# Narrow blocks of the first expert folded in three separate steps, and another order for the second expert's splits and the last index product

## The chip, the core and the metric

The kernel runs on one core of one Trainium2 chip. The metric is the device time of one execution in microseconds (us). The core's engines are TensorE (PE; its weight loads are listed as PEld), VectorE (DVE), ScalarE (ACT), GpSimd (POOL) and SyncE (SP). Each engine works through its own queue in the order in which the program gave the instructions out; engines wait for each other by semaphores.

## What is computed

Two stages: an attention with decay over 4 batches and 8 heads of 576 positions by 64, and on its 2304 rows of 512 a mixture of 8 experts in which each row goes to one expert.

```python
ret = scale * (q @ k.T) * Dmat            # Dmat: gamma_h ** (i - j), lower triangle
x = (ret @ v) as rows of 8 * 64
logits = x @ w_gate
e = argmax(logits); gate_w = softmax(logits)[e]
slot = position among the rows of expert e   # at most 2 * 2304 / 8 = 576
h = relu(rows_of_e @ w1[e])               # 512 -> 1024
y = h @ w2[e]                             # 1024 -> 512
out[row] = gate_w * y[its slot]
```

## The kernel before

**Two stages on one queue of work.** The attention runs over 18 tiles of 128 rows. Routing is computed in four groups of tiles (4, 4, 5 and 5): logits, the best expert (DVE: `lg`, `mx`, `cand`, `first`, `ohs`), ranks within experts (PE), then an index product (PE, L538, from `hot` and `vals` into the bank `psl`) that makes the list of rows of each expert, and a weight product (PE, L596, from `hot` and `wals`) that makes the list of gate weights. The last group's routing is interleaved with the first expert. The order of all instructions is written out by hand: a manual schedule keeps the order in which the code gives them out, and each engine keeps that order in its own queue.

**Precision.** A weight or activation is held as two f16 numbers, a high and a low part (`wh` and `wl`, `hh` and `hl`), and each product is made of three matmuls: high by high, high by low, low by high.

**Weights.** An expert has four quarters of 1 MB, loaded by SP (L238, `fetch`) into four buffers `raw`. Each quarter is split in two halves: `high` is an activation on ACT (L262, writes `wh`), `low` an operation on DVE (L270, writes `wl`, 128x1024). When `low` of a quarter's second half has been given out, the buffer's next load is given out behind it. An expert thus has eight parts 0 to 7; the text calls a `high` and a `low` of one part a split.

**One expert** (`run`). Eight blocks f of 12 matmuls (L901 to L903) each fill one of three rotating PSUM banks `ph`; ACT writes `hh` from it (L906), DVE `hl` (L907). Then `full(r)` multiplies 128 rows at a time (24 matmuls, L927 to L929, one of four rotating banks `py`; ACT scales to `ot`, L914, and POOL scatters the rows to the output, L918). The rest of less than 128 rows goes to `narrow(r, n)`: matmuls with 64 or 32 columns (L947) write partial sums into different partitions of two banks x and y. Its result must be folded: ACT copies from y to `both` and `more` (L996 to L1002), DVE adds x and `both` (L1003) and `more` (L1004), then ACT scales to `ot` (L1007, L1009) and POOL scatters. How many rows an expert has is known at run time only; `sized` chooses among widths by branches (L700).

**The order of experts.** Expert 0 comes in two parts: its first 256 slots (one `full` and one `narrow` of 128) while the last routing is under way, and its second part (112 slots, one `narrow`). Experts 1 to 7 follow. What else is to be given out during `run` stands in a table `pieces`: the key (f,) means behind block f (from 0), the key (r, f) behind step f of the product of row block r. The table of the first part gives out, among others, the routing steps `go` (routing of the last group; the last one of them is the last index product), `rows_late` (gathers of expert 0's second part and of expert 1, ranks), `w1st` and `w2nd` (gate weights of the last two groups), and the `hi` and `lo` of expert 1. `turn_late` transposes the second part's rows: ACT copies one half to `exT`, DVE the other (L1071). Expert 2's splits during expert 1, and later ones, follow `SPLITS_AT`.

**Held output.** For expert 0's first part `run` gets a list `held`: the scaling and scattering of its rows need the gate weights, which come late. `held` collects these steps (one for `full`, one for `narrow`), and `let_go`, given out behind block 4 of the second part, runs them all. The copies and additions of the fold itself are given out at once behind the narrow block.

Of the kernel before, what the change touches and what calls it, by code (L numbers as in the profile page):

```python
# [10 lines left out]
F32 = mybir.dt.float32  # L11
# [7 lines left out]
P = 128  # L19
# [20 lines left out]
    ((2,), (3,), (4,), (5,), (6,), (7,), (0, 3), (1, 3)),  # L40
# [3 lines left out]
HALF = 64  # L44
# [42 lines left out]
def retention_moe(ctx, tc, q, k, v, w_gate, w1, w2, capacity, consts, where, out):  # L87
# [796 lines left out]
    def run(w, xT, c0, T, pieces, idc, wtc, held=None, used=None, widths=(), at=1):  # L884
# [53 lines left out]
        def narrow(r, n):  # L938
# [52 lines left out]
            both = ob_p.tile([P, DM], F32, tag="both", name="both", bufs=1)  # L991
            more = ob_p.tile([P, DM], F32, tag="more", name="more", bufs=1)
            ot = ob_p.tile([P, DM], F32, tag="ot", name="ot")
            few = min(n, HALF)
            part = min(n, HALF + QUARTER)
            nc.scalar.copy(both[:few], y[HALF:HALF + few])  # L996
            if n > HALF:
                a, z = HALF, part
                nc.scalar.copy(both[a:z], y[0:z - a])  # L999
            else:  # L1000
                a, z = 0, min(n, QUARTER)
            nc.scalar.copy(more[a:z], y[QUARTER:QUARTER + z - a])  # L1002
            nc.vector.tensor_tensor(out=both[:part], in0=x[:part], in1=both[:part], op=ALU.add)  # L1003
            nc.vector.tensor_tensor(out=both[a:z], in0=both[a:z], in1=more[a:z], op=ALU.add)  # L1004

            def leave():
                nc.scalar.activation(ot[:part], both[:part], AF.Copy, scale=wtc(r)[:part])  # L1007
                if n > part:
                    nc.scalar.activation(ot[part:n], x[part:n], AF.Copy, scale=wtc(r)[part:n])  # L1009
                send(r, n, ot)  # L1010

            if held is None:
                leave()
            else:
                held.append(leave)
# [29 lines left out]
    def hi(*parts):  # L1045
        return sp(1, *parts, do=high)
# [30 lines left out]
    def let_go():  # L1077
        while held:
            held.pop(0)()
# [6 lines left out]
    for bank in phs.banks[:2]:  # L1086
# [3 lines left out]
               lambda: low(0, 2, 1), fetch, fetch],  # L1090
        (1,): [lambda: cross(NTI - 1, pys.banks[-1]), lambda: logits(NTI - 2)],
# [4 lines left out]
        (7,): [go, rows_late, w1st, w1st],  # L1096
        (0, 0): hi(0),
        (0, 1): hi(1, 2),
        (0, 2): hi(3),
        (0, 3): hi(4) + [w2nd],  # L1100
# [3 lines left out]
        (0, 7): [turn_late, w1st, w2nd] + hi(5) + lo(1),  # L1104
# [3 lines left out]
        (1,): lo(2),  # L1108
# [3 lines left out]
        (5,): lo(3),  # L1112
        (6,): [w2nd],
        (7,): hi(6),
        (0, 3): lo(4) + hi(7),
        (0, 7): lo(5),
    })
    rest = {(0,): lo(6), (1,): lo(7)}
    for e in range(1, E):
        pieces = {(p,): [] for p in range(KF)}  # L1120
        if e == 1:
            pieces.update(rest)
# [107 lines left out]
```

## Time and profile before

| | |
|---|---|
| median of 3 runs | 330.56 us (330.53 to 330.68) |
| the profiled execution | 332.88 us |
| its span, first to last instruction | 331.0 us |
| mean granted TensorE clock | 0.988 |
| PE / PEld busy | 308.3 / 216.6 us |
| DVE / ACT / POOL busy | 195.8 / 188.6 / 108.3 us |
| moved by DMA | 69.03 MB |

Busy time is the union of an engine's instructions; that of PE is modelled from pipelined matmuls. PE is busy for 93% of the span, so the question of each stretch is what ends its few idle times. The attention fills the time up to about 109 us, expert 0's first part with the last routing 109 to 130.5, its second part 130.5 to 142.8, expert 1 to 173.5, and the other six experts follow.

### The profile page before, as it was taken

What the parts mean: (1) busy time and instruction counts of PE and PEld (TensorE: products, weight loads), DVE (VectorE), ACT (ScalarE), POOL (GpSimd) and SP (SyncE); (2) the same over time, 40 slices, a digit from 0 to 9 for tenths busy, and PEclk for the clock granted to TensorE, in tenths of its full rate; (3) what the DMA queues carried; (4) which work ended last, traced back from release to release, by engine and by line L of the source; (5) the groups of instructions that cost most, each with busy time, mean ns of one, the idle gap of its engine ahead of it and who ended that gap; (6) DMA issues with size and microseconds to landing.
All of it is one profiled execution on the core that took longest, in us unless ns stands there. A gap on an engine that the chain in (4) does not pass through costs nothing. (4 is left out here: it accounts for less than half of the span.)

```text
span 331.0 us, 8265 instructions
## 1 busy us (share of the span) xinstructions
PE 308.3 (93%) x3227; PEld 216.6 (65%) x3228; DVE 195.8 (59%) x416; ACT 188.6 (57%) x333; POOL 108.3 (33%) x116
## 2 busy tenths in 40 slices
PE   8889999999998899779999999999999999999960
PEld 4678999899978775546447547647646647648620
DVE  4435587988579789759818815915914934912300
ACT  2567776876668466647557637736735736733310
POOL 1375353565409513116015012512414212421120
PEclk9999999999999999999999999999999999999995
DMA  8999999999967887986997993966995995721010
GB/s 176 197 200 218 273 247 267 233 231 244 239 222 159 286 321 156 221 268 201 217 327 228 305 260 120 357 151 227 363 208 201 293 191 209 154 58 38 3 36 33
DMA packets 97514, 69.03 MB, mean 209 GB/s; under 512 B 79975, under 2 KB 80359, under 8 KB 97456
## 3 DMA queue, kind: packets, MB, share of 16 engines
q1 hardware_dynamic: 93728, 58.08, 68.1%
q0 software_dynamic: 3728, 10.13, 8.9%
q8 instruction: 42, 0.69, 0.9%
q14 instruction: 16, 0.13, 0.1%
HBM read 53.58 MB, written 10.05 MB: 192 GB/s over the span
## 5 line engine op out<-in xcount | busy, mean ns | idle before, releaser
L270 DVE SCALAR_TENSOR_TENSOR wl<-raw,wh 128x1024 f16<-128x1024 f32 x62 | 76.9, 1241 | 8.6 <-ACT wh L262 8.1
L903 PE MATMUL ph<-exT,wl 128*128 128x296 f16 (+6 forms) x288 | 78.2, 278 | 1.7 <-issue 1.7
L901 PE MATMUL ph<-exT,wh 128*128 128x296 f16 (+6 forms) x288 | 78.2, 278 | 1.4 <-DVE hl L907 1.3
L902 PE MATMUL ph<-exT,wh 128*128 128x296 f16 (+6 forms) x288 | 78.2, 278 | 0.0
L918 POOL DMA_INDIRECT out<-ot,idx x24 | 26.0, 1084 | 140.9 <-ACT ot L914 75.3
L262 ACT ACTIVATE wh<-raw 128x1024 f16<-128x1024 f32 x64 | 66.6, 1052 | 1.6 <-DMA raw<-in_w 1.5
L907 DVE SCALAR_TENSOR_TENSOR hl<-ph,hh 128x256 f16<-128x256 f32 (+8 forms) x72 | 32.3, 453 | 36.2 <-ACT hh L906 36.1
L906 ACT ACTIVATE hh<-ph 128x256 f16<-128x256 f32 (+8 forms) x72 | 29.0, 411 | 29.9 <-PE ph L903 25.2
L927 PE MATMUL py<-wh,hh 128*128 128x512 f16 x120 | 45.5, 380 | 0.2 <-PEq L700 0.2
L929 PE MATMUL py<-wh,hl 128*128 128x512 f16 x120 | 45.5, 379 | 0.0
L928 PE MATMUL py<-wl,hh 128*128 128x512 f16 x120 | 45.5, 379 | 0.0
L901 PEld LDWEIGHTS <-wh 128*128 128x128 f16 x288 | 28.2, 98 | 10.4 <-issue 3.3
L902 PEld LDWEIGHTS <-wh 128*128 128x128 f16 x288 | 28.2, 98 | 8.7 <-issue 1.7
L903 PEld LDWEIGHTS <-wl 128*128 128x128 f16 x288 | 28.2, 98 | 6.5
L734 POOL DMA_INDIRECT xg<-xr,idx x24 | 28.0, 1167 | 12.4 <-issue 5.8
L914 ACT ACTIVATE ot<-py,sws 128x512 f32<-128x512 f32 x14 | 9.6, 687 | 39.3 <-PE py L929 31.6
L282 POOL TENSOR_TENSOR ks<-kn,cst 128x512 f32<-128x512 f32 x17 | 17.9, 1051 | 40.1 <-DMA kn<-in_k 31.8
L1003 DVE TENSOR_TENSOR both<-py,both 96x512 f32<-96x512 f32 (+6 forms) x9 | 6.2, 684 | 33.9 <-ACT both L999 19.0
L333 DVE TENSOR_TENSOR pm<-pp,cst 128x512 f32<-128x512 f32 x36 | 23.2, 684 | 2.5 <-PE pp L328 1.1
L947 PE MATMUL py<-wl,hh 128*64 128x512 f16 (+2 forms) x80 | 23.0, 381 | 0.0
L947 PE MATMUL py<-wh,hl 128*64 128x512 f16 (+2 forms) x80 | 22.0, 380 | 0.3 <-DVE hl L907 0.2
L947 PE MATMUL py<-wh,hh 128*64 128x512 f16 (+2 forms) x80 | 22.3, 382 | 0.0
(179 smaller groups left out, 485.3 us busy)
## 6 DMA issues: line engine op xcount, KB each, us to landing
raw<-in_w SPq DMA_DIRECT2D x32, 1024.0 KB, 6.5
xr<-xrow SPq DMA_DIRECT2D x18, 256.0 KB, 8.9
qn<-in_q SPq DMA_DIRECT2D x16, 256.0 KB, 5.3
vn<-in_v SPq DMA_DIRECT2D x16, 256.0 KB, 5.0
kn<-in_k SPq DMA_DIRECT2D x15, 256.0 KB, 4.8
kn<-in_k SPq DMA_DIRECT2D x6, 128.0 KB, 3.9
qn<-in_q SPq DMA_DIRECT2D x4, 128.0 KB
vn<-in_v SPq DMA_DIRECT2D x4, 128.0 KB
```

What stands on the lines that cost most here:

```text
L262: nc.scalar.activation(hv, raw[:, c], AF.Copy, scale=SW)
L270: nc.vector.scalar_tensor_tensor(out=lv, in0=raw[:, c], scalar=SW, in1=hv, op0=ALU.mult, op1=ALU.subtract)
L734: nc.gpsimd.indirect_dma_start(out=self.rows[:n, r, :].bitcast(I32), out_offset=None, in_=xr[:, :], in_offset=bass.IndirectOffsetOnAxis(ap ...
L901: nc.tensor.matmul(ph[:, :T], w.h1[:, kd, cols], xT[:, kd, z], start=(kd == 0), stop=False)
L902: nc.tensor.matmul(ph[:, :T], w.h1[:, kd, cols], xT[:, KD + kd, z], start=False, stop=False)
L903: nc.tensor.matmul(ph[:, :T], w.l1[:, kd, cols], xT[:, kd, z], start=False, stop=(kd == KD - 1))
L906: nc.scalar.activation(hh[:, f, :T], ph[:, :T], AF.Relu)
L907: nc.vector.scalar_tensor_tensor(out=hl[:, f, :T], in0=ph[:, :T], scalar=0.0, in1=hh[:, f, :T], op0=ALU.max, op1=ALU.subtract)
L927: nc.tensor.matmul(py[:n], hh[:, f, cols], w.h2[:, f, :], start=(f == 0), stop=False)
L928: nc.tensor.matmul(py[:n], hh[:, f, cols], w.l2[:, f, :], start=False, stop=False)
L929: nc.tensor.matmul(py[:n], hl[:, f, cols], w.h2[:, f, :], start=False, stop=(f == KF - 1))
L947: nc.tensor.matmul(to, a[:, f, cols], b[:, f, :], start=start, stop=stop, skip_group_check=True)
```

## The change

The fold of a narrow block becomes three steps: `take` (the copies to `both`), `add` (the copy to `more` and both additions) and `leave` (scaling and scatter). With a list `held` they are appended to it, otherwise they run at once. `let_go` now runs one held step per call, and it is called at seven places: four in the second part of expert 0 and three in expert 1. The second part gets the list too. Expert 1's splits 1 to 7 are given out later than before, expert 2's splits at other places of expert 1's run; the last index product with `rows_late` and two steps of weights moves from behind block 7 to behind the first step of the first product; the logits of one tile and a `low` of expert 0 change places. No arithmetic changes.

```diff
 SPLITS_AT = (
-    ((2,), (3,), (4,), (5,), (6,), (7,), (0, 3), (1, 3)),
+    ((6,), (7,), (0, 1), (0, 4), (0, 6), (1, 0), (1, 3), (1, 6)),
...
-            nc.scalar.copy(both[:few], y[HALF:HALF + few])
-            if n > HALF:
-                a, z = HALF, part
-                nc.scalar.copy(both[a:z], y[0:z - a])
-            else:
-                a, z = 0, min(n, QUARTER)
-            nc.scalar.copy(more[a:z], y[QUARTER:QUARTER + z - a])
-            nc.vector.tensor_tensor(out=both[:part], in0=x[:part], in1=both[:part], op=ALU.add)
-            nc.vector.tensor_tensor(out=both[a:z], in0=both[a:z], in1=more[a:z], op=ALU.add)
+            a, z = (HALF, part) if n > HALF else (0, min(n, QUARTER))
+            got = {}
+
+            def take():
+                both = got["both"] = ob_p.tile([P, DM], F32, tag="both", name="both", bufs=1)
+                nc.scalar.copy(both[:few], y[HALF:HALF + few])
+                if n > HALF:
+                    nc.scalar.copy(both[a:z], y[0:z - a])
+
+            def add():
+                both = got["both"]
+                more = ob_p.tile([P, DM], F32, tag="more", name="more", bufs=1)
+                nc.scalar.copy(more[a:z], y[QUARTER:QUARTER + z - a])
+                nc.vector.tensor_tensor(out=both[:part], in0=x[:part], in1=both[:part], op=ALU.add)
+                nc.vector.tensor_tensor(out=both[a:z], in0=both[a:z], in1=more[a:z], op=ALU.add)
...
-            if held is None:
-                leave()
-            else:
-                held.append(leave)
+            for step in (take, add, leave):
+                if held is None:
+                    step()
+                else:
+                    held.append(step)
...
     def let_go():
-        while held:
-            held.pop(0)()
+        held.pop(0)()
...
         (0,): [lambda: logits(NTI - 3), lambda: blank_bank(phs.banks[2], max(CAPS)),
-               lambda: low(0, 2, 1), fetch, fetch],
-        (1,): [lambda: cross(NTI - 1, pys.banks[-1]), lambda: logits(NTI - 2)],
+               lambda: logits(NTI - 2)],
+        (1,): [lambda: cross(NTI - 1, pys.banks[-1]), lambda: low(0, 2, 1), fetch, fetch],
...
-        (7,): [go, rows_late, w1st, w1st],
-        (0, 0): hi(0),
+        (0, 0): [go, rows_late, w1st, w1st] + hi(0),
...
-        (0, 3): hi(4) + [w2nd],
+        (0, 3): [w2nd],
...
-        (0, 7): [turn_late, w1st, w2nd] + hi(5) + lo(1),
+        (0, 7): [turn_late, w1st, w2nd] + hi(4),
...
     fast(0, n_early, len(blocks[0]) - n_early, {
-        (1,): lo(2),
         (2,): [w2nd],
         (3,): [lambda: load_length(1)],
         (4,): [let_go],
-        (5,): lo(3),
         (6,): [w2nd],
-        (7,): hi(6),
-        (0, 3): lo(4) + hi(7),
-        (0, 7): lo(5),
-    })
-    rest = {(0,): lo(6), (1,): lo(7)}
+        (7,): lo(1, 2) + [let_go],
+        (0, 3): lo(3) + [let_go],
+        (0, 7): [let_go],
+    }, held)
+    behind = {
+        (0,): lo(4) + [let_go], (1,): hi(5) + lo(5), (2,): [let_go], (3,): hi(6) + lo(6), (4,): [let_go],
+        (5,): hi(7) + lo(7),
+    }
```

DVE's queue from the slot weights (`wals`) of the last group through the first blocks of expert 0's second part, before. `wl_2496` is a weight of expert 1, `both<-py_2105` the fold of the first part's narrow block, `hl` of 112 columns the second part's:

```order
L589 TENSOR_TENSOR wals<-cell,pws 128x5x24 x3
L270 SCALAR_TENSOR_TENSOR wl_2496<-raw,wh_2495 128x1024
L1003 TENSOR_TENSOR both<-py_2105,both 96x512
L1004 TENSOR_TENSOR both<-both,more 32x512
L907 SCALAR_TENSOR_TENSOR hl<-ph_2100,hh 128x112
L907 SCALAR_TENSOR_TENSOR hl<-ph_2098,hh 128x112
L270 SCALAR_TENSOR_TENSOR wl_2496<-raw,wh_2495 128x1024
L907 SCALAR_TENSOR_TENSOR hl<-ph_2099,hh 128x112
```

The same queue from the last two `hl` of the second part on, after the change:

```order
L907 SCALAR_TENSOR_TENSOR hl<-ph_2100,hh 128x112
L644 TENSOR_TENSOR pr<-place,swt 128x147
L648 TENSOR_REDUCE sws<-pr 128x21
L907 SCALAR_TENSOR_TENSOR hl<-ph_2098,hh 128x112
L270 SCALAR_TENSOR_TENSOR wl_2496<-raw,wh_2495 128x1024
L700 UNCONDITIONAL_BRANCH
L270 SCALAR_TENSOR_TENSOR wl_2496<-raw,wh_2495 128x1024 x2
L1006 TENSOR_TENSOR both<-py_2105,both 96x512
L700 UNCONDITIONAL_BRANCH x3
L1007 TENSOR_TENSOR both<-both,more 32x512
L907 SCALAR_TENSOR_TENSOR hl<-ph_2099,hh 128x384
```

The split and the two additions that stood between `wals` and the first `hl` of 112 columns, and the split between the second and the third, now stand behind the eighth.

ACT's queue behind block 4 of expert 0's second part, before (`ph_2098` to `ph_2100` are the three banks of the blocks; `ot` are the held outputs of the first part):

```order
L906 ACTIVATE hh<-ph_2098 128x112
L914 ACTIVATE ot<-py_2104,swt 128x512
L1007 ACTIVATE ot<-both,swt 96x512
L1009 ACTIVATE ot<-py_2105,swt 32x512
L906 ACTIVATE hh<-ph_2099 128x112
L906 ACTIVATE hh<-ph_2100 128x112
L906 ACTIVATE hh<-ph_2098 128x112
```

The same place after the change:

```order
L906 ACTIVATE hh<-ph_2098 128x112
L914 ACTIVATE ot<-py_2104,swt 128x512
L906 ACTIVATE hh<-ph_2099 128x112
L906 ACTIVATE hh<-ph_2100 128x112
L906 ACTIVATE hh<-ph_2098 128x112
L998 COPY both<-py_2106 64x512
L1000 COPY both<-py_2106 32x512
```

Two of the three outputs moved behind the eighth `hh`, and so did the copies of the first part's fold.

DVE's queue at the end of expert 1, before (`wl_3126` belongs to expert 2, `hl` of 348 columns is expert 2's first):

```order
L270 SCALAR_TENSOR_TENSOR wl_3126<-raw,wh_3125 128x1024
L700 UNCONDITIONAL_BRANCH x3
L1003 TENSOR_TENSOR both<-py_2106,both 96x512
L1004 TENSOR_TENSOR both<-both,more 32x512
L270 SCALAR_TENSOR_TENSOR wl_3126<-raw,wh_3125 128x1024
L907 SCALAR_TENSOR_TENSOR hl<-ph_2098,hh 128x348
```

The same place after the change:

```order
L270 SCALAR_TENSOR_TENSOR wl_3290<-raw,wh_3289 128x1024 x2
L270 SCALAR_TENSOR_TENSOR wl_3292<-raw,wh_3291 128x1024
L700 UNCONDITIONAL_BRANCH x3
L1006 TENSOR_TENSOR both<-py_2106,both 96x512
L1007 TENSOR_TENSOR both<-both,more 32x512
L270 SCALAR_TENSOR_TENSOR wl_3292<-raw,wh_3291 128x1024 x3
L907 SCALAR_TENSOR_TENSOR hl<-ph_2098,hh 128x348
```

Three splits instead of one now stand ahead of expert 1's narrow fold in its products, and three instead of one between that fold and expert 2's first `hl`.

## Rows read from the trace of the kernel before

**Rows 1.** Stretches: length, busy us (instructions) of PE, PEld, DVE, ACT, POOL, clock, DMA, GB/s

```profile
130.50:137.30 6.80, 5.43 (x103) 5.04 (x101) 5.49 (x15) 4.25 (x11) 0.47 (x1) 1.00 1.12 129
142.80:149.85 7.05, 5.35 (x39) 3.52 (x37) 3.61 (x7) 4.00 (x7) 0.91 (x1) 1.00 0.75 254
173.50:320.00 146.50, 146.35 (x986) 89.34 (x984) 75.66 (x101) 78.59 (x121) 37.09 (x34) 1.00 0.65 192
```

**Rows 2.** Waits of PE from 108.5 to 150: releaser, us, times, longest

```profile
PE ph L903 <- issue: 1.7, 1, 1.7
PE ph L901 <- DVE hl L907: 1.3, 2, 1.1
PE psl L538 <- DVE hot L531: 0.7, 1, 0.7
PE psl L440 <- DVE xT L420: 0.6, 1, 0.6
```

**Rows 3.** Timeline of DVE, last routing: start, us, instruction [idle before]

```profile
111.11 2.52 DVE L270 SCALAR_TENSOR_TENSOR wl<-raw,wh 128x1024 f16<-128x1024 f32 x1
...
113.89 0.41 DVE L420 COPY xT<-py 128x512 f16<-128x512 f16 x1
...
116.16 0.20 DVE L481 TENSOR_TENSOR ohs<-cand,first 128x40 f16<-128x40 f32 x1
```

**Rows 4.** Timeline of PE, expert 0's second part and its narrow block's start

```profile
130.49 0.22 PE L901 MATMUL ph<-exT,wh 128*128 128x112 f16 x1
...
132.28 0.33 PE L596 MATMUL psl<-wals,hot 128*128 128x72 f16 x5
133.73 0.21 PE L901 MATMUL ph<-exT,wh 128*128 128x112 f16 x1 [1.13 <-DVE hl L907]
...
137.33 0.40 PE L947 MATMUL py<-wh,hh 128*64 128x512 f16 x1
```

**Rows 5.** Timeline of DVE beside it

```profile
129.75 0.38 DVE L1071 COPY exT<-py 128x448 f16<-128x448 f16 x1
...
130.77 1.22 DVE L270 SCALAR_TENSOR_TENSOR wl<-raw,wh 128x1024 f16<-128x1024 f32 x1
131.90 0.68 DVE L1003 TENSOR_TENSOR both<-py,both 96x512 f32<-96x512 f32 x1
132.69 0.68 DVE L1004 TENSOR_TENSOR both<-both,more 32x512 f32<-32x512 f32 x1
133.40 0.46 DVE L907 SCALAR_TENSOR_TENSOR hl<-ph,hh 128x112 f16<-128x112 f32 x2
```

**Rows 6.** Timeline of PE: expert 1's first block, its narrow and second full product

```profile
142.80 0.32 PE L901 MATMUL ph<-exT,wh 128*128 128x340 f16 x1
...
163.78 0.40 PE L947 MATMUL py<-wh,hh 128*64 128x512 f16 x1
...
168.33 0.39 PE L927 MATMUL py<-wh,hh 128*128 128x512 f16 x1
```

**Rows 7.** Timeline of ACT, expert 0's second part

```profile
136.45 0.71 ACT L1007 ACTIVATE ot<-both,swt 96x512 f32<-96x512 f32 x1
...
137.89 0.26 ACT L906 ACTIVATE hh<-ph 128x112 f16<-128x112 f32 x1
```

**Rows 8.** Timeline of PE, block 3 of expert 1

```profile
148.85 0.30 PE L903 MATMUL ph<-exT,wl 128*128 128x340 f16 x1 [1.70 <-issue]
```

**Rows 9.** DMA queues from 146.4 to 147.6: packets, MB, share of 16 engines

```profile
q1 hardware_dynamic: 220, 0.45, 98.8%
q8 instruction: 1, 0.02, 5.7%
```

**Rows 10.** Timeline of DVE, first `hl` of expert 2

```profile
175.82 0.52 DVE L907 SCALAR_TENSOR_TENSOR hl<-ph,hh 128x348 f16<-128x348 f32 x1 [0.85 <-ACT hh L906]
```

**Rows 11.** Timeline of PE, start of expert 2's fourth block

```profile
178.35 0.30 PE L901 MATMUL ph<-exT,wh 128*128 128x316 f16 x1
```

**Rows 12.** Weight loads of the page: count, KB each, median us to landing

```profile
raw<-in_w SPq DMA_DIRECT2D x32, 1024.0 KB, 6.5
```

More of the change, by code (lines that the diff above doesn't have):

```diff
@@ L990, in narrow @@
             piece(r, KF - 1)
-            both = ob_p.tile([P, DM], F32, tag="both", name="both", bufs=1)
-            more = ob_p.tile([P, DM], F32, tag="more", name="more", bufs=1)
-            ot = ob_p.tile([P, DM], F32, tag="ot", name="ot")
             few = min(n, HALF)
             part = min(n, HALF + QUARTER)
-            nc.scalar.copy(both[:few], y[HALF:HALF + few])
-            if n > HALF:
-                a, z = HALF, part
-                nc.scalar.copy(both[a:z], y[0:z - a])
-            else:
-                a, z = 0, min(n, QUARTER)
-            nc.scalar.copy(more[a:z], y[QUARTER:QUARTER + z - a])
-            nc.vector.tensor_tensor(out=both[:part], in0=x[:part], in1=both[:part], op=ALU.add)
-            nc.vector.tensor_tensor(out=both[a:z], in0=both[a:z], in1=more[a:z], op=ALU.add)
+            a, z = (HALF, part) if n > HALF else (0, min(n, QUARTER))
[11 more added lines that the diff above has]
+                nc.vector.tensor_tensor(out=both[a:z], in0=both[a:z], in1=more[a:z], op=ALU.add)
             def leave():
-                nc.scalar.activation(ot[:part], both[:part], AF.Copy, scale=wtc(r)[:part])
+                ot = ob_p.tile([P, DM], F32, tag="ot", name="ot")
+                nc.scalar.activation(ot[:part], got["both"][:part], AF.Copy, scale=wtc(r)[:part])
                 if n > part:
@@ L1121, in retention_moe @@
         if e == 1:
-            pieces.update(rest)
+            pieces.update(behind)
         if e + 1 < E:
```

## The prediction

> **What bounds the kernel now.** I read the stretches first [rows 1]. From 173.5 us to the end of the products TensorE (PE) is busy 146.35 of 146.50 us at a granted clock of 1.00, so whatever brings PE to 173.5 earlier is handed to the end one for one: no later stage has slack to swallow it, and the tail (320 to 331) only follows PE. The idle time of PE that this change can touch lies before: 1.37 us in 130.50:137.30 and 1.70 us in 142.80:149.85. Next I read who ends those waits [rows 2]: 1.3 us end with VectorE's (DVE's) `hl`, 0.7 with `hot`, 0.6 with a copy of `xT`, and 1.7 with nothing that the profile knows. Busy time of PE is modelled, so the terms below are taken from starts of matmuls, not from busy sums. DVE and ScalarE (ACT) are the engines to watch: both are in-order queues, and what PE waits for stands in them behind work that nobody needs yet.
>
> The sum is made on the profiled execution (span 331.0 us, its own time 332.88 us) and subtracted from the median of the runs, 330.56 us; the 2 us between the profiled time and the median are taken as the same before and after. A measurement of this kernel tells about 0.2% (0.66 us) from no change.
>
> **Term 1, the routing and the start of expert 0's second part: -0.3 us.** Three edits belong here. (a) The split of the weights given out after block 1 moves behind block 2. Today it runs 2.52 us [rows 3], and the copy of `xT` behind it starts at 113.89; PE waits 0.6 us for that copy [rows 2]. With the copy ahead, PE gains that. But the split (1.2 us where it is undisturbed, [rows 5]) then stands directly in front of the routing chain, whose result `ohs` starts at 116.16 [rows 3]: I place the copy at 113.3, the split at 113.7 and `ohs` 0.6 us later than now. PE's rank products, which today follow block 5 at once, then wait for it, and PE is where it was. Net nothing. (b) The last index product is given out after the first three matmuls of the first 128-row product instead of before them. 24 such matmuls take 5.17 us (168.33 to 173.50, [rows 1, 6]), three take 0.65; they fill the 0.7 us wait for `hot`, and the product itself is no later, since it waits for `hot` either way. PE is 0.65 us ahead from there. (c) It can't keep that: block 1 of the second part reads `exT`, whose second half DVE copies at 129.75 for 0.38 us [rows 5], in a queue that is busy without a gap from the rank products on and that this change does not shorten before that copy. So the block starts at about 130.2 instead of 130.49 [rows 4]. The bounds are 0 (the routing becomes later) and -0.65.
>
> **Term 2, the eight blocks of the second part: -1.8 us.** They take 130.49 to 137.33, 6.84 us [rows 4]. Three of them run undisturbed, 130.49 to 132.28: 0.60 each. Eight make 4.8, the five weight products (L596) and the step to the narrow block 0.3: 5.05. The rest is wait, and the rows name it: at 133.73 PE had waited 1.13 us for `hl`, and DVE's `hl` at 133.40 stands behind a split at 130.77 and the two additions of the first part's narrow block at 131.90 and 132.69 [rows 4, 5]. Three copies on ACT stand before `hh` in the same way. In the new order nothing of this is ahead of the second part's `hl`: folding is held, the splits 1, 2 and 3 come after block 8. Of the held steps only one `ot` remains inside the blocks (0.7 us on ACT after block 5), and four blocks later nothing of PE depends on it. The split that now precedes them (part 0) ends where it ends today, before 129.75. Bounds: -1.5 to -1.8.
>
> **Term 3, the narrow block behind it: -0.9 us.** It takes 137.33 to 142.80, 5.47 us; expert 1's narrow block, the same two forms with the same 48 matmuls and no wait, takes 163.78 to 168.33, 4.55 us [rows 4, 6]. The difference is PE standing for `hl` of blocks 7 and 8, which are late because ACT ran three `ot` activations before their `hh` (137.89) [rows 6, 7]. Two of those three are now behind the narrow block. Bounds: -0.6 to -0.9.
>
> What the moved work needs instead: splits 1 to 3 of expert 1 run behind `hl` of block 8, at about 136.2 to 139.7 in the new time; expert 1 needs the last of them at the twelfth matmul of its block 1, about 141.4. Cover 1.7 us. Its first `hl` ends near 143.4, since ACT first leaves the folded block; PE needs its bank at block 4, near 145.0. Cover 1.6 us. The second fold and the splits 5 to 7 then share the eight blocks of expert 1, in which DVE before did five splits of expert 2; these move into the two products of 128 rows and the blocks just before them. On GpSimd's queue the gathers of expert 2 now come before the second part's store, so nothing of it waits longer; on SyncE's queue the loads for expert 2 start later by about 2 us and are used some 10 us later than before.
>
> **Term 4, the wait without a name: -1.2 us.** In block 3 of expert 1 PE stands 1.7 us, to 148.85, for no semaphore [rows 2, 8]. In the 1.2 us before the wait's visible end a transfer of the instruction queue runs, while the loads hold the DMA engines at 98.8% [rows 9]. I read it as code that arrived late. Bounds: 0 (it waits as before, relative to the program) and -1.7 (the code is there). I take -1.2, near the lower end: about 60 blocks later in this kernel are built from the same branches and pass without a wait [rows 1], so the place in the program alone doesn't make it; what is special is three weight loads in a row that were issued while the second part's blocks ran, and that now start after split 1, behind the blocks.
> The Trainium skill, Runtime: NRT & Kernel Launch, section Instruction fetch mechanics, says that a taken branch to a target outside the two resident pages must fetch the page before execution goes on. By that rule the wait hangs on the place in the program, which this change leaves alone, and would stay: 327.6 us, the first rival. The trace agrees that a fetch lies there; that blocks of the same build pass without one speaks against it.
>
> Sum: 0.3 + 1.8 + 0.9 + 1.2 = 4.2 us; 330.56 - 4.2 = 326.4 us.
>
> **Rivals.** *The code wait stays.* Terms 1 to 3 only, 3.0 us: 327.6. For it: a code transfer lies beside the wait, and PE reaches the same place sooner, with less time to fetch. Against it: the blocks without a wait.
> *DVE stays the bound of the second part.* If `hl` of blocks 7 and 8 are still late (the slot weights' two operations stand between them in the new order too), term 3 and half of term 2 go, and the code wait stays: 330.56 - 0.3 - 0.9 = 329.4. Against it: these two operations are short, while the additions alone are 1.5 us with their gaps [rows 5].
> *It does not do what it says.* If the wait at 133.73 moves one by one to expert 1's blocks, because ACT's folding there delays `hh` by more than the 1.6 us of cover, nothing is left: 330.6. Against it: three free PSUM banks lie between `hh` and PE there, and ACT is idle over a third of that stretch (4.00 of 7.05 us busy, [rows 1]).
> *Slower: expert 2 starts late.* Three splits instead of one now stand on DVE between expert 1's narrow block and expert 2's first `hl`. That `hl` ends at 176.34 and PE needs its bank at 178.35 [rows 10, 11]; two more splits of 1.22 less the 0.85 us that DVE idles there make it 177.93 [rows 5, 10]: 0.4 us of cover, in a phase in which a block gives DVE an `hl` of 0.52 and a split of 1.22 and PE some 1.7 (0.60 for 112 columns, scaled to 316), so that a delay is not recovered but also not repeated. Each us beyond is one us lost. It decides from 4.2 + 0.4 = 4.6 us (3.4 us where the code wait stays), that is if the last weight load of expert 2 lands that late in front of the splits: it is issued once the transposes of expert 2 are out, near 155, and is needed near 171, against 6.5 us that such a load takes [rows 12]. With 6 us of delay the kernel takes 332.0.
>
> **How the numbers follow.** Forecast 326.4 with 0.50; code wait stays, 327.6, 0.27; DVE stays the bound, 329.4, 0.11; nothing gained, 330.6, 0.06; slower, about 332, 0.06. The lower end is term 4 at -1.7 and term 1 at -0.65 with some of the remaining small gaps: 330.56 - 5.05 = 325.5, taken as 325.2. The upper end is the third case, 329.4. Left out are the last two cases and a little below: under 0.2. Faster by over 0.2% are the first three: 0.88; within 0.2% 0.06; slower 0.06.
>
> **What would show it.** Term 1: the rank products near 117.0 and block 1 of the second part near 130.2. Term 2: no PE wait of 1.1 us behind the weight products, and narrow matmuls starting 5.0 to 5.1 us after the part's first block. Term 3: 4.5 to 4.6 us for that narrow block. Term 4: the third block of expert 1 without a wait over 0.6 us; a wait of 1.7 us or more there means the first rival. Expert 2's fourth block right behind its third speaks against the last rival. The forecast is wrong if expert 1's first block starts later than 140.5, or if PE shows a new wait between 140 and 180.

## The result, and the profile after

The changed kernel takes 327.65 us (median of 20 runs) beside 330.54 us of the kernel before (20 runs): a ratio of 0.9914, 95% interval 0.989 to 0.9937, that is 2.1 to 3.6 us less, 2.8 in the middle. A second measurement on another occasion gave 0.9907 (0.9876 to 0.9939). Forecast were 326.4 us and a range from 325.2 to 329.4. The kernel became faster, but by about two thirds of the 4.2 us forecast; 327.6 us, the time of the first rival, is what came out, though not by that rival's mechanism, as the runs show.

The profiled execution of the changed kernel took 328.75 us, its span is 327.0 us. The stretches that answer to [rows 1] (length, then busy us and instructions of PE, PEld, DVE, ACT, POOL, clock, DMA share, GB/s):

```profile
131.30:136.30 5.00, 5.00 (x103) 4.90 (x101) 2.78 (x14) 2.32 (x8) 0.53 (x1) 1.00 1.13 165
140.85:147.90 7.05, 7.05 (x52) 4.81 (x50) 4.40 (x7) 5.20 (x9) 3.04 (x3) 1.00 0.79 311
169.70:316.20 146.50, 146.28 (x985) 89.33 (x984) 78.09 (x103) 79.97 (x123) 36.15 (x34) 1.00 0.69 202
```

PE has no idle time left in the second part's blocks (5.00 of 5.00 us; before 5.43 of 6.80) nor at the start of expert 1 (7.05 of 7.05; before 5.35 of 7.05). The late stages are as full as before. The waits of PE from 110 to 170 us, which answer to [rows 2] (engine, line and releaser; us in total, times, longest):

```profile
PE psl L485 <- DVE ohs L481: 0.4, 1, 0.4
PE ph L901 <- issue: 0.2, 1, 0.2
```

The 1.3 us for `hl`, the 0.7 for `hot`, the 0.6 for `xT` and the 1.7 for nothing are gone; 0.4 for `ohs` and 0.2 for nothing are new. PE's timeline at the second part, for [rows 4] and [rows 6] (start, duration, instruction):

```profile
131.33 0.22 PE L901 MATMUL ph<-exT,wh 128*128 128x112 f16 x1
...
133.27 0.21 PE L901 MATMUL ph<-exT,wh 128*128 128x112 f16 x1
...
136.32 0.40 PE L947 MATMUL py<-wh,hh 128*64 128x512 f16 x1
...
140.87 0.32 PE L901 MATMUL ph<-exT,wh 128*128 128x340 f16 x1
```

The fourth block follows the weight products at once (133.27, no wait in brackets). Blocks take 4.99 us (before 6.84), the narrow block 4.55 (before 5.47).

**A ruler for all runs.** The time at which expert 0's first matmul starts was 106.7 to 111.9 us in the fourteen profiles of this study, although no edit lies ahead of it. The spans of after, after_again, load_early and load_late (the last two are the changed kernel with one small edit each) lie within 3.8 us, counted from that matmul within 0.3: most of this spread comes from the attention stage. From that matmul on, a stage without a new wait repeats to a few hundredths, the long rest to some tenths. So experiments are read by stages, from starts of matmuls: first part (to the second part's first block), second part's blocks, its narrow block, expert 1's eight blocks, its products, the rest to the end of the span. In us:

| kernel | first part | blocks | narrow | expert 1's blocks | its products | rest |
|---|---|---|---|---|---|---|
| before, first profile | 21.56 | 6.84 | 5.47 | 15.70 | 15.02 | 157.48 |
| after, first profile | 21.01 | 4.99 | 4.55 | 13.85 | 15.01 | 157.27 |
| before_again | 21.55 | 6.85 | 5.47 | 14.12 | 15.01 | 157.19 |
| after_again | 20.98 | 4.99 | 4.55 | 13.85 | 15.01 | 157.41 |
| fold_only | 22.42 | 5.43 | 4.55 | 13.85 | 15.02 | 157.11 |
| order_only | 21.02 | 6.19 | 4.55 | 14.11 | 15.01 | 157.25 |
| term1_only | 21.61 | 6.76 | 5.46 | 14.11 | 15.02 | 157.19 |
| splits23_behind | 21.55 | 6.29 | 4.55 | 14.70 | 15.01 | 157.67 |
| index_back | 22.44 | 4.98 | 4.55 | 13.85 | 15.02 | 156.92 |
| splits2_back | 21.09 | 4.98 | 4.55 | 15.31 | 15.01 | 156.89 |
| load_early | 20.87 | 4.99 | 4.55 | 13.85 | 15.02 | 157.20 |
| load_late | 21.01 | 4.99 | 4.55 | 13.85 | 15.01 | 157.06 |
| flood | 21.39 | 4.99 | 4.55 | 14.74 | 15.02 | 157.46 |
| split_behind_ohs | 21.59 | 4.98 | 4.55 | 13.85 | 15.02 | 156.96 |

The first two rows differ by 5.4 us, the two medians by 2.8. That gap is the question of the experiments.

### The profile page after: what moved, and what is told of

It is laid out like the page before. It is cut to its first block, busy times and chain, and to the rows that moved or that the text cites. A ratio compares the mean times of both kernels' runs of the same rounds, so it can differ in the third digit from the quotient of the medians.

```text
span 327.0 us, 8261 instructions
## 1 busy us (share of the span) xinstructions
PE 307.5 (94%) x3227; PEld 216.6 (66%) x3228; DVE 197.5 (60%) x416; ACT 188.3 (58%) x333; POOL 107.4 (33%) x116
## 5 line engine op out<-in xcount | busy, mean ns | idle before, releaser
L918 POOL DMA_INDIRECT out<-ot,idx x24 | 24.4, 1015 | 138.2 <-ACT ot L914 52.3
L927 PEld LDWEIGHTS <-hh 128*128 128x128 f16 x120 | 11.7, 98 | 15.4 <-issue 3.0
```

The lines of the kernel that those rows point to most:

```text
L927: nc.tensor.matmul(py[:n], hh[:, f, cols], w.h2[:, f, :], start=(f == 0), stop=False)
```

## The experiments

### Each kernel once more

The kernel before and the changed kernel, unchanged.

> The kernel before, unchanged, profiled once more. Theory (the wait of 1.7 us is an event of single executions; with loads that start early the code transfer that belongs to expert 1 starts 0.1 us before to 3.7 us after expert 1's first matmul, and only past about +1.7 PE waits): first part, second part and narrow block 21.56, 6.84, 5.47 as in the first profile; expert 1's blocks 13.9 to 14.2 without that wait at odds of three to one, transfer between -0.1 and +3.7. Rival (the wait belongs to the program): 15.70 again.

> The changed kernel, unchanged, beside the next run on the same chip. Stages as in its first profile: 21.0, 4.99, 4.55, 13.85, 15.01; the code transfer of expert 1 at -1.3 to -2.0; median 0.8 to 1.3% under that of the kernel before. Rival (code waits are as frequent here): a wait of over 1 us in expert 1's blocks.

The kernel before repeats every stage within 0.02 us but one: expert 1's blocks take 14.12 us instead of 15.70. The stretch that had 1.70 us of idle time in [rows 1], and PE's waits, in this second profile:

```profile
142.80:149.85 7.05, 6.94 (x51) 4.59 (x49) 3.60 (x7) 5.56 (x9) 2.18 (x2) 1.00 0.73 262
```

```profile
PE ph L901 <- DVE hl L907: 1.1, 1, 1.1
PE psl L538 <- DVE hot L531: 0.7, 1, 0.7
PE psl L440 <- DVE xT L420: 0.5, 1, 0.5
PE py L947 <- DVE hl L907: 0.3, 2, 0.2
```

The waits for `hl`, `hot` and `xT` are there again; the wait for nothing is not. It was an event of one execution. That execution was also a long one: 332.88 us against a median of 330.56, while this one took 330.90. The totals alone settle little: the 17 runs of the same kernel beside this second profile have a median of 332.13 us. What expert 1's blocks still have over the changed kernel (14.12 against 13.85) is one wait of 0.27 us, in front of the fourth block (148.25), where DVE's first `hl` of expert 1 ends at 148.20, behind the fold.

The changed kernel repeats its stages too. Between these two undisturbed profiles, from expert 0's first matmul on, lie 0.57 + 1.86 + 0.92 + 0.27 - 0.22 = 3.40 us, inside the interval of the runs (2.1 to 3.6 for the first measurement, 2.0 to 4.1 for the second). The 5.4 us between the first profiles lie outside both, and none of the eight profiles with the changed kernel's loads has that wait; so most executions of the kernel before were without it too.

### The two halves of the change

fold_only has the three steps and the seven places of `let_go`, with every split where it was:

```diff
-        (7,): hi(6),
-        (0, 3): lo(4) + hi(7),
-        (0, 7): lo(5),
-    })
-    rest = {(0,): lo(6), (1,): lo(7)}
+        (7,): hi(6) + [let_go],
+        (0, 3): lo(4) + hi(7) + [let_go],
+        (0, 7): lo(5) + [let_go],
+    }, held)
+    rest = {(0,): lo(6) + [let_go], (1,): lo(7), (2,): [let_go], (4,): [let_go]}
```

> Only the fold is changed (three steps, let go one by one at the seven places); the splits, the index product and SPLITS_AT stand as before. The stages are counted by starts of matmuls: second part's blocks (6.84 us before, 4.99 after), its narrow block (5.47 and 4.55), expert 1's eight blocks (15.70 and 13.85). Theory (fold and outputs in front of hl cost terms 2 and 3; weight loads that start near 135.5 delay the code and cost term 4): blocks 5.0 to 5.3, narrow 4.6 to 5.0, expert 1's blocks 15.4 to 15.9 with one wait of 1.3 us or more for no semaphore, because the loads start as early as before. Rival (the code wait came from the lateness of PE itself or is chance): expert 1's blocks 13.9, no wait.

order_only has all the rest, and folds as before (copies and additions at once, all outputs let go behind block 4):

```diff
-        (7,): lo(1, 2) + [let_go],
-        (0, 3): lo(3) + [let_go],
-        (0, 7): [let_go],
-    }, held)
+        (7,): lo(1, 2),
+        (0, 3): lo(3),
+    })
```

> Everything of the change but the fold: copies and additions at once, outputs let go all at once behind block 4 of the second part. Theory: the three copies on ACT and the two additions on DVE still stand in front of the second part's first hh and hl, so the blocks take 5.6 to 6.0 us; three outputs in front of hh of block 6 make the narrow block 5.3 to 5.5; the loads start behind block 8, so expert 1's blocks take 13.9 without a wait. Rival (the split at the head of DVE's queue alone was the cause of term 2): blocks 5.0 and narrow 4.6.

The second part's blocks: 5.43 us with the fold alone, 6.19 with the order alone, 4.99 with both. Of the 1.85 us the fold's steps alone give 1.41, the order alone gives 0.65; the two overlap. With the order alone PE still stands for `hl` in front of the fourth block:

```profile
132.64 0.21 PE L901 MATMUL ph<-exT,wh 128*128 128x112 f16 x1 [1.05 <-DVE hl L907]
```

So the split at the head of DVE's queue was not the cause by itself; the fold in front of `hl` was enough for 1.05 us.

The narrow block is the miss: 4.55 us in both. The order alone leaves the three outputs in a row on ACT, in front of `hh` of block 6, and still the narrow block has no wait. Over the runs of its measurement fold_only has 0.9925 of the time before (0.9893 to 0.9958), order_only 0.9955 (0.9922 to 0.9987).

On the code wait fold_only spoke against the theory first: its loads start early, at 137.00, and expert 1's blocks take 13.85 us, no wait. But it has such a wait elsewhere, in the first part, where neither theory had placed one:

```profile
119.65 0.27 PE L901 MATMUL ph<-exT,wh 128*128 128x220 f16 x1 [1.56 <-issue]
```

### What made the narrow block late

The kernel before with two low halves moved behind the second part's last block; the outputs and the fold stay:

```diff
-        (1,): lo(2),
         (2,): [w2nd],
...
-        (5,): lo(3),
         (6,): [w2nd],
-        (7,): hi(6),
+        (7,): lo(2, 3) + hi(6),
```

> The kernel before with the low halves 2 and 3 of expert 1 moved from behind blocks 1 and 5 of the second part to behind its last block; the split at the head (part 1) and the fold stay. Theory (the splits, not the outputs on ACT, made hl of the last blocks late, since the outputs wait for gate weights that DVE computes behind a split): the wait of 1.1 us in the fourth block stays (blocks 6.2 to 6.7), the narrow block takes 4.55 to 4.7 instead of 5.47. Rival (three outputs in front of hh on ACT): narrow block 5.3 to 5.5. Code wait: the first load starts as in the kernel before; 13.9 for expert 1's blocks if the wait comes in some executions only, 15.7 if it belongs to the order.

The narrow block takes 4.55 us, with all three outputs in front of `hh`. ACT's timeline in this kernel (second part from 132.48) shows them in a row, as [rows 7] did, but they start right behind the fifth `hh`:

```profile
137.10 0.26 ACT L906 ACTIVATE hh<-ph 128x112 f16<-128x112 f32 x1 [0.33 <-PE ph L903]
137.26 0.68 ACT L914 ACTIVATE ot<-py,swt 128x512 f32<-128x512 f32 x1
137.83 0.71 ACT L1007 ACTIVATE ot<-both,swt 96x512 f32<-96x512 f32 x1
138.57 0.68 ACT L1009 ACTIVATE ot<-py,swt 32x512 f32<-32x512 f32 x1
139.28 0.58 ACT L906 ACTIVATE hh<-ph 128x112 f16<-128x112 f32 x3
```

So the outputs take as long as before (2.1 us), and they make `hh` of block 6 as late as before: it starts 0.51 us behind the narrow block's first matmul (139.28 less 138.77), in the kernel before 0.56 us (137.89 less 137.33). The first output's wait of 0.49 us for the gate weights in the kernel before (135.86) does not count there, since PE is as late. What differs is DVE behind `hh`. In the kernel before a split stands between `hl` of block 6 and `hl` of block 7, and PE's narrow block waits for the last two `hl`:

```profile
138.18 0.27 DVE L907 SCALAR_TENSOR_TENSOR hl<-ph,hh 128x112 f16<-128x112 f32 x1 [1.99 <-ACT hh L906]
138.37 1.22 DVE L270 SCALAR_TENSOR_TENSOR wl<-raw,wh 128x1024 f16<-128x1024 f32 x1
139.50 0.27 DVE L907 SCALAR_TENSOR_TENSOR hl<-ph,hh 128x112 f16<-128x112 f32 x1
...
140.62 0.40 PE L947 MATMUL py<-wh,hl 128*64 128x512 f16 x1 [0.18 <-DVE hl L907]
```

In splits23_behind the two `hl` stand together:

```profile
139.57 0.46 DVE L907 SCALAR_TENSOR_TENSOR hl<-ph,hh 128x112 f16<-128x112 f32 x2 [1.90 <-ACT hh L906]
```

`hl` of block 7 starts 1.0 us behind the narrow block's first matmul there (139.77), 2.2 us in the kernel before. The outputs alone are harmless (here and in order_only), and so is the split alone (fold_only keeps it, with one output instead of three, and does not wait): late `hh` and the split behind it together cost the 0.9 us. The two splits then pile up in expert 1, where PE waits 0.69 us for `hl` (14.70).

### Term 1 and the index product

term1_only is the kernel before with the routing edits alone:

```diff
-               lambda: low(0, 2, 1), fetch, fetch],
-        (1,): [lambda: cross(NTI - 1, pys.banks[-1]), lambda: logits(NTI - 2)],
+               lambda: logits(NTI - 2)],
+        (1,): [lambda: cross(NTI - 1, pys.banks[-1]), lambda: low(0, 2, 1), fetch, fetch],
...
-        (7,): [go, rows_late, w1st, w1st],
-        (0, 0): hi(0),
+        (0, 0): [go, rows_late, w1st, w1st] + hi(0),
```

> The kernel before with the two edits of term 1 alone: logits and one low half of expert 0 exchanged, the last index product behind the first step of the first product. Theory (DVE's queue sets the second part's hl whatever PE does): first part 21.0 us (21.56 before), but the second part's blocks 7.3 to 7.4 (6.84 before), so that the sum stays at 28.4; narrow block 5.4 to 5.5. Rival (PE's lead is kept): 21.0 and 6.84. On the code wait: weight loads as in the kernel before; if the wait of 1.7 us belongs to that order, expert 1's blocks take 15.7 again; if it comes in some executions only, 13.9 is the likelier.

First part and blocks together take 28.37 us, as before (28.40). The sum is as the theory said, the parts are not: the wait for `hot` is gone, but this execution waited 0.52 us for gathered rows (`xg`, at 127.59) in the first part, and so the blocks had nothing to give back. Without that wait the first part would be 21.1. Whether the lead would then have been lost in the blocks is not shown by this run.

index_back is the changed kernel with the last index product back behind block 7:

```diff
+        (7,): [go, rows_late, w1st, w1st],
-        (0, 0): [go, rows_late, w1st, w1st] + hi(0),
+        (0, 0): hi(0),
```

> The changed kernel with the last index product, the late gathers and two steps of weights back behind block 7. Theory: PE waits 0.6 to 0.7 us for hot again, first part 21.5 to 21.7 (21.01 after), the other stages as after (4.99, 4.55, 13.85, 15.01). Rival (the wait for hot is hidden by DVE's queue further on): first part 21.0.

Its time settles nothing on `hot`: a code wait fell in just ahead of it and covered it, and the first part took 22.44 us.

```profile
120.20 0.27 PE L901 MATMUL ph<-exT,wh 128*128 128x220 f16 x1 [1.76 <-issue]
```

Its trace says more. `hot` ends 11.86 us after expert 0's first matmul, as in the changed kernel (11.87); in the kernel before it was 12.35. In the changed kernel PE starts its first product at 11.70. So behind block 7 PE would wait some 0.2 us for `hot` (an estimate from these two times), not the 0.6 to 0.7 expected: the exchange (a) had already brought `hot` forward by 0.5.

### Where the code comes late

Three runs work on the code wait. load_early and load_late are the changed kernel with another place for part 1 of expert 1, whose end frees the buffer of expert 2's first load:

```diff
+        (5,): lo(1),
         (6,): [w2nd],
-        (7,): lo(1, 2) + [let_go],
+        (7,): lo(2) + [let_go],
```

> The changed kernel with one low half (part 1 of expert 1, whose end lets the first weight load of expert 2 start) moved from behind block 8 of the second part to behind block 6, so that this load starts about 1.5 us earlier, at about 137.5, ahead of the code transfer at 138.84. Nothing else moves. Theory (loads in front of the code transfer delay the code): expert 1's blocks 15 to 16 us with a wait for no semaphore of over 1 us, blocks of the second part 5.0 to 5.3. Rival (place in the program, or chance): 13.9, no wait.

```diff
-        (7,): lo(1, 2) + [let_go],
+        (7,): lo(2, 1) + [let_go],
```

> The changed kernel with the low halves 1 and 2 of expert 1 exchanged behind block 8, so that the first weight load of expert 2 starts 1.2 us later. Theory (in the changed kernel the code transfer at 138.84 is only 0.14 us ahead of the first load, so that some executions lose the race): stages as after (4.99, 4.55, 13.85) in the profile, and a median 0.3 to 1.0 us under that of the changed kernel (327.65). Rival (no race): the same median within the noise.

load_early did not do what it was made for. The low half ended at 133.4 us, but the load left at 135.40, where the next low half ended: against expert 1's first matmul 1.7 us ahead, as in the changed kernel (1.9). load_late moved it to 1.3 us ahead. Neither has a wait, and their ratios, 0.9904 (0.9867 to 0.9941) and 0.9897 (0.9851 to 0.9942), can't be told from that of the changed kernel. The gain that was expected of load_late is not shown.

flood does move the queues: the changed kernel with four copies of 512 KB from device memory to device memory ahead of the loads.

```diff
+    def flood():
+        for i in range(4):
+            nc.sync.dma_start(
+                out=spill[i][:, :].rearrange("(k p) f -> p k f", p=P),
+                in_=w2[0, i * 2 * P:(i + 1) * 2 * P, :].rearrange("(k p) f -> p k f", p=P),
+            )
...
-        (0, 7): [turn_late, w1st, w2nd] + hi(4),
+        (0, 7): [turn_late, w1st, w2nd, flood] + hi(4),
```

> The changed kernel with four extra copies of 512 KB inside device memory, given out on SP behind expert 1's transposes, so that the DMA queues are full from about 134 us (the copied data is used by nothing). Theory (full DMA queues delay code, and PE stands when the delay passes the slack): the code transfer that starts 1.3 to 2.0 us before expert 1's first matmul in the six kernels with later loads starts at +0.9 us or later, and expert 1's blocks take 14.2 to 17 us with a wait for no semaphore. Rival (the transfer's time is set by the program alone): -1.3 to -2.0 and 13.85. The stages before as after.

Expert 1's blocks take 14.74 us, 0.89 more, with one wait at the start of the seventh block, which the view puts down to DVE:

```profile
151.96 0.31 PE L902 MATMUL ph<-exT,wh 128*128 128x340 f16 x1 [0.69 <-DVE wl L271]
```

The changed kernel speaks against that name (line numbers of flood are one higher). Its same `wl` runs from 150.96 to 152.18, while its seventh block started near 151.26 and waited for nothing, so PE does not depend on it. The `hl` that this block does need ended at 150.8 in flood. What PE waited for shows in the rows of its sequencer, which the profile lists under PEld. A run-time branch (L700, L701 in flood) takes 0.21 us in the median of every profile. In flood the one that begins at 148.88 takes 2.6 us, to 151.49 (the row gives its least, middle and longest duration in ns):

```profile
L701 PEldq COMPARE_BRANCH  x1: 2615/2615/2615, 148.9 to 148.9; - x1
```

It ends 1.5 us after a code transfer (149.06 to 149.99; 8.4 us after expert 1's first matmul, where the same one in the two profiles of the changed kernel comes 4.7 and 5.3 us after). Two short branches follow, to 151.90, and PE goes on at 151.96. The waits of fold_only and index_back look the same: a branch of 2.28 us to 119.59 and one of 1.98 us to 120.14, each 1.4 us behind the end of a code transfer that started 7.4 us after expert 0's first matmul; in the twelve other profiles that transfer starts at 4.8 to 5.4. So I read these three as waits for code at a branch; that the transfers end them rests on the same 1.4 to 1.5 us in all three. The wait of 1.70 us in the first profile of before is not at a branch: none of PE's branches lies between 144.28 and 148.87. It fell in the middle of a block, and ended 1.3 us behind the transfer's end (147.57). A long branch need not cost PE: fold_only has another of 1.82 us at 150.04, and PE does not stand there.

What the fourteen profiles give together is the time at which the code transfer (16 KB, instruction queue) that falls nearest to expert 1's first matmul starts, counted from that matmul. In all of them 2050 matmuls lie ahead of it, so the same code should be due there:

| kernels | expert 2's first load (or flood) starts | code transfer starts |
|---|---|---|
| before, before_again, term1_only, fold_only, splits23_behind | 5.2 to 10.1 us ahead | +3.67, +1.41, +1.50, +0.93, -0.07 |
| flood | 7.4 us ahead | +2.02 |
| the other eight, with the loads of the changed kernel | 0.9 to 2.4 us ahead | -1.26 to -2.03 |

The two groups don't overlap. The DMA queues from 140.8 to 146.4 us in the first profile of before, where the code should have come (queue: packets, MB, share of 16 engines), held no instruction row at all, and the data queue was at 81.6%:

```profile
q1 hardware_dynamic: 454, 1.42, 81.6%
```

From 138.8 to 139.9 in the changed kernel the code has the queues for itself:

```profile
q8 instruction: 1, 0.02, 5.4%
```

With loads in front of it the code comes 1 to 6 us later. Only flood changes nothing but the queues, and it is one run (some 4 us later than in the two profiles of the changed kernel); the five profiles above it also have another order on DVE and ACT. Of these five only the longest delay, +3.67, made PE stand in that block; the other four passed. Full queues make the wait possible; in four of five executions of that order it did not come.

### Expert 2's splits, and one step further

splits2_back is the changed kernel with the old first row of SPLITS_AT.

```diff
-    ((6,), (7,), (0, 1), (0, 4), (0, 6), (1, 0), (1, 3), (1, 6)),
+    ((2,), (3,), (4,), (5,), (6,), (7,), (0, 3), (1, 3)),
```

> The changed kernel with the first row of SPLITS_AT as before, so that expert 2's splits begin behind block 2 of expert 1, together with the folds and expert 1's last splits. In expert 1's eight blocks DVE would have 8 hl of 0.55, 4 splits of expert 1, 2 folds of 1.4 and 6 splits of expert 2 of 1.22: 19.4 us against PE's 13.85. Theory (the splits had to leave for the folds to fit): expert 1's blocks 15 to 17 us with waits for hl. Rival (DVE has room, or the raw weights come too late to matter): 13.85. The stages before it as after.

Expert 1's blocks take 15.31 us, 1.46 more, with waits of 0.29 and 0.84 us for `hl`:

```profile
154.67 0.30 PE L901 MATMUL ph<-exT,wh 128*128 128x340 f16 x1 [0.84 <-DVE hl L907]
```

The later places for expert 2's splits pay for the fold's move into expert 1; without them 1.5 of the 3.4 us between the undisturbed profiles would go.

split_behind_ohs moves expert 0's low half one block further, behind the routing steps that make `ohs`:

```diff
-        (1,): [lambda: cross(NTI - 1, pys.banks[-1]), lambda: low(0, 2, 1), fetch, fetch],
-        (2,): [lambda: logits(NTI - 1), go, go],
+        (1,): [lambda: cross(NTI - 1, pys.banks[-1])],
+        (2,): [lambda: logits(NTI - 1), go, go, lambda: low(0, 2, 1), fetch, fetch],
```

> The changed kernel with expert 0's low half and its two loads moved one block further, from behind block 1 to behind block 2's two routing steps, so that the split no longer stands on DVE in front of ohs. Theory (edit (a) of term 1 is worth nothing since the split still delays the rank products by 0.36 us, and the split is not needed before the first product): rank products 7.3 to 7.5 us after expert 0's first matmul (7.81 after), no wait for ohs, first part 20.4 to 20.7 us (21.01), the other stages as after. Rival (DVE's queue sets the first part's end through later steps): first part 21.0.

The rank products start 7.27 us after expert 0's first matmul, as expected, and the wait for `ohs` is gone. It comes back at the index product:

```profile
124.36 0.22 PE L538 MATMUL psl<-vals,hot 128*128 128x48 f16 x2 [0.55 <-DVE hot L531]
```

The first part takes 21.59 us, 0.6 more than in the changed kernel, of which 0.35 is another wait without a name (130.72). From `lg` to `hot` DVE's queue is one chain; a split in front of `ohs` costs PE 0.36 us, one between `ohs` and `hot` costs 0.55. Its ratio, 0.9901 (0.9866 to 0.9937), stands beside 0.9907 of the changed kernel on the same chip. No version faster than the changed kernel was found.

## Why the prediction was right or wrong

**The bound** held. Everything that PE gained before expert 2 reached the end: the products of expert 1 take 15.01 us and the rest 157.2 to 157.4 in both kernels' second profiles.

**Term 1** was forecast at -0.3 and measured -0.57. Step (a) had the right picture (the wait for `xT` becomes one for `ohs`), with 0.17 us gained instead of nothing. Step (b) fits: no wait for `hot` in either profile of the changed kernel; but it had only some 0.2 us of that wait left to save (the estimate at index_back), for (a) had taken the rest. Step (c) was wrong, and through step (a). From `hot` to the copy of `exT` DVE's queue is 9.29 us long in both kernels; but `hot` itself starts 0.48 us earlier. In the kernel before DVE stood 0.60 us in front of `hl` of block 5, because PE's wait for `xT` had made that block late; `hh` of it starts 8.18 us after expert 0's first matmul before and 7.48 after, and the wait is gone:

```profile
117.53 0.42 DVE L907 SCALAR_TENSOR_TENSOR hl<-ph,hh 128x256 f16<-128x256 f32 x1 [0.60 <-ACT hh L906]
```

The same row after the change:

```profile
118.43 0.42 DVE L907 SCALAR_TENSOR_TENSOR hl<-ph,hh 128x256 f16<-128x256 f32 x1
```

So the copy starts 20.34 us after expert 0's first matmul instead of 20.82 (130.66 less 110.32, 129.75 less 108.93), and PE kept 0.55 us (21.56 less 21.01), where 0.3 had been expected. In term1_only, with the edits of this term alone, it starts at 20.32.

**Term 2**, -1.8, measured -1.86, with the mechanism as told: the fold and the splits in front of `hl`, worth 1.41 and 0.65 us alone.

**Term 3**, -0.9, measured -0.92, was right in size and had half of the cause. The three outputs on ACT do make `hh` of the last blocks late, but that alone costs nothing: two runs with all three in place have no wait. It took the split on DVE between `hl` of blocks 6 and 7 as well (138.37), which the prediction left out.

**What the moved work needs.** The cover for expert 1's first `hl` was thinner than I had it, 1.0 us instead of 1.6: DVE's `hl` starts at 144.52 because ACT first waits for the fold's additions, which stand behind three splits.

```profile
137.64 3.49 DVE L270 SCALAR_TENSOR_TENSOR wl<-raw,wh 128x1024 f16<-128x1024 f32 x3
...
144.52 0.56 DVE L907 SCALAR_TENSOR_TENSOR hl<-ph,hh 128x384 f16<-128x384 f32 x1 [2.01 <-ACT hh L906]
```

It was enough. With the fold at once, in before_again, the same `hl` costs PE 0.27 us; this gain was not in the sum.

**Term 4**, -1.2, is the step that failed. In the profiles without a code wait it is 0. The text took a wait of the profiled execution off the median, and said that the 2 us between that execution and the median could be taken as the same before and after. They could not: 332.88 us was an execution with the wait, and the median is one of executions mostly without, as the interval of the medians shows beside the two pairs of profiles. The argument that the later blocks of the same build (53, not 60) pass without a wait was sound, but what it says is that the wait is chance, and a chance that one of five profiles shows is worth some 0.3 us (an estimate, a fifth of 1.58), not 1.2. Two readings of the term's rows were off too: the transfer of [rows 9] ends at 147.57, 1.3 us ahead of the wait's end and not beside it, and of the three loads in a row only the first was issued while the second part's blocks ran (135.46; the others at 139.71 and 142.99). Without term 4 the forecast would have read 327.6 us, for the measured 327.65. That the terms 1 to 3 came out 0.35 larger in the profiles than forecast (3.35), beside 2.8 in the medians, lies within the intervals; code waits in the first part, which two of the fourteen profiles show, may take part of it, and that stays open.

The **first rival** gave the right time for another reason: it said that the wait stays. It does not stay in the changed kernel's profiles; it was not in the median before. By the rule of the Trainium skill (Runtime: NRT & Kernel Launch, section Instruction fetch mechanics) that a branch out of the resident pages must wait for a fetch, the wait would hang on the place; two profiles of the same program, with and without it, show that the place alone does not make it, and in the one that has it PE stood at no branch. The branches of flood, fold_only and index_back, which took 2.0 to 2.6 us, are nearer to the rule.

The **slower rival** (expert 2 starts late) did not come. Three splits in a row stand there as foreseen, and DVE waited 2.58 us for ACT's `high` ahead of them:

```profile
169.96 3.50 DVE L270 SCALAR_TENSOR_TENSOR wl<-raw,wh 128x1024 f16<-128x1024 f32 x3 [2.58 <-ACT wh L262]
173.38 0.51 DVE L907 SCALAR_TENSOR_TENSOR hl<-ph,hh 128x348 f16<-128x348 f32 x1
```

The rival had put such a delay down to the weight load. In this profile it is ACT's queue: the `high` follows the outputs of expert 1's narrow block at once and waits for no load.

```profile
168.17 0.68 ACT L1013 ACTIVATE ot<-py,sws 32x512 f32<-32x512 f32 x1
168.87 2.95 ACT L262 ACTIVATE wh<-raw 128x1024 f16<-128x1024 f32 x3
```

The first `hl` ends at 173.89, PE needs its bank at 174.56: 0.7 us of cover, where 0.4 had been reckoned. The margin is thin, and expert 1's fold on ACT sets it.

**One sign** was ill made. Expert 1's first block starts at 140.87, later than the 140.5 that was to show the forecast wrong, but only because expert 0's first matmul came at 110.32 instead of 108.93. Counted from that matmul it starts at 30.55 us instead of 33.87.

## What to carry to other kernels

A wait that the view puts down to no engine is to be looked for in a second profile before it enters a sum; a profiled execution that is slower than the median by about that wait is a hint that the median lacks it, no more, where runs spread by as much for other reasons. A wait in an in-order chain is to be followed back over all engines: two small delays that are harmless alone (late `hh`, a split behind it) can cost time together. Results of an optional kind (outputs, folds, splits for a later stage) belong in an in-order queue behind what the matmuls wait for, and what must make room for them further on has to be moved with them: here expert 2's splits, worth 1.5 us in expert 1's blocks. Where run times spread by more than the effect, count stages from a common matmul instead of comparing totals.

## What the runs showed of the hardware

Code transfers of 16 KB share the DMA engines with data. With loads of 1 MB or copies of 512 KB started 5 to 10 us ahead of the stage, the transfer at expert 1 started between 0.1 us before and 3.7 us after its first matmul (six profiles); with the loads 0.9 to 2.4 us ahead, 1.3 to 2.0 us before it in all eight. PE stood 0.69 to 1.76 us in four cases (148.85 in the first profile of before, 119.65 in fold_only, 120.20 in index_back, 151.96 in flood), in the last three behind a branch that took 2.0 to 2.6 us instead of 0.21, and its sequencer or PE went on 1.3 to 1.5 us after the end of a transfer. The same attention code brought expert 0's first matmul anywhere from 106.7 to 111.9 us at a granted clock of 0.98 to 0.99 over the span; what sets that stays open.
